# Lightning attention and a two-layer MLP on one core: the third pair of chunks as two units, with natural token order, later output stores and whole visits

## The chip, the cores and the metric

The kernel runs on one core of one Trainium2 chip. The metric is the device time of one execution in microseconds. The core's engines work side by side, each on its own queue in a fixed order: TensorE (PE, matmuls, with its weight loads as PEld), VectorE (DVE), ScalarE (ACT), GpSimd (POOL) and SyncE (SP), which only issues DMAs here. An engine that waits at the head of its queue holds up all that is queued behind it. Sixteen DMA engines serve all queues together.

## What is computed

The reference first does a causal linear attention with a decay per head, on q, k, v of shape (4, 8, 768, 64), in blocks of 64 tokens with a running state, and then an MLP on the 3,072 tokens with 512 channels:

```python
for b in range(nb):                      # blocks of 64 tokens
    intra = einsum('bhic,bhjc->bhij', qb, kb) * Dmask
    intra = einsum('bhij,bhjd->bhid', intra, vb)
    inter = einsum('bhid,bhde->bhie', qb * lam_pow, kv_state)
    out[:, :, sl] = intra + inter
    kv_state = lam_block * kv_state + einsum('bhsd,bhse->bhde', kb * rev_pow, vb)
...
h = x @ w_in                             # x: 3072 x 512, w_in: 512 x 2048
g = where(h >= 1, h, where(h <= -1, 0, (h + 1)**2 / 4))
out = g @ w_out                          # w_out: 2048 x 512
```

The kernel scales q by lam to the power of the position and k by its inverse (position counted from the middle of the sequence), so that the decays vanish from scores and state, and it computes in bf16 with fp32 sums.

## The kernel before

**Tiles and stages.** The tokens of the four sequences are cut into 24 chunks of 128 (6 to a sequence) and six stages of 512 tokens. For a stage, `f_l1` (L621) forms ph = w_in^T xT in pieces of 512 columns, `f_r` (L629, ACT) writes relu(h + 1) out of PSUM, `f_g` (L637, L640, L645, DVE) makes the activation gT, `f_l2` (L654) sums y over 16 pieces of gT and w_out, `f_y` (L679, ACT) copies y to an output buffer osb, and `f_out` (L686, L688 from POOL's queue, L690 and L675 from SP's) stores it. There are eight osb buffers (OB), two PSUM banks of ph and two of py: the copy of y number n + 8 needs the store of y number n to have landed, and an L621 group needs the L629 of the group two before it.

**Attention in units.** Tokens 0 to 511 (the first four chunks) come as four units of 256 tokens by 4 heads: unit 0 and 1 are the two head halves of tokens 0 to 255, units 2 and 3 of tokens 256 to 511. A unit is loaded with two neighbouring tokens side by side, in 512-byte runs (`e_load`, L317), so token 2p + j lies in partition p. It goes through scaling (`e_cast`, L330), transposes (`e_t`, L344), copies (`e_tc`, L351), scores (`e_s`, L388), mask (`e_m`, L396), state updates into the PSUM bank pu (`e_upd`, L364), copies of the state (`e_st`, L379), the state's part of the output (`e_sp`, L408), a drain of TensorE for units 2 and 3, the scores' part (`e_o`, L423), and a copy of the result to xT (`e_x`, L434). The tokens of a unit stand in xT with all even ones before all odd ones, and the stores of stage 0 put them back: each is two DMAs of 64 rows (L686).

**Chunks 4 and 5** (tokens 512 to 767, the end of the first sequence) are loaded by `f_load` (L441) in 256-byte runs, one head's row of one token each. k is scaled on DVE and q on POOL (L465), v cast on ACT (L458); `f_t` (L476) transposes on TensorE, `f_tc` copies (L481), `f_s` (L571) makes scores, `f_m` (L578) masks them, and `f_o` (L586, L590, L595) makes the output and, for chunk 4, the state update. `f_x` (L610) copies the output to xT, `f_ub` (L606) the state.

**Chunks 6 to 23** are loaded in the same 256-byte runs; k and q are scaled on POOL (L468), v cast on ACT (L458), and one DMA on SP's queue transposes k and q together (`f_tx`, L485, kqT). TensorE handles them in visits: `f_visit2(c)` multiplies scores by v (L542), adds the state's part (`f_sp`, L526), and then does `f_ahead(c + 1)`: `f_sp` and the scores of the next chunk (`f_sd`, L507) and the key-value products of the one after (`f_kv`, L515). DVE adds these up (`f_st`, L552 and L554), ACT casts the state (`f_sc`, L559), DVE masks the scores (L580), ACT copies the output (`f_xh`, L563). For c in SPLIT = (9, 11), `f_ahead` is a visit of its own some groups later.

**The order of the work.** A planner (`run_plan`) gives each piece an engine, a cost, needs and a due time, and from that writes down one order for every queue. What it emits is fixed; on the chip only the semaphores of the tiles and of the buffers count, so a need that stands only in a piece's list orders the plan and adds no wait. SP's queue holds all loads in order, with the transposes of kqT between them; a load of chunk c reuses the buffer of chunk c - 6. The first load of chunk 4 is held until the last but one slice of w_out has landed. POOL's queue holds the casts of k and q and the stores of stages 0 to 4; GL, LDMA, Y_TO and the like are the planner's numbers. The projections of stage 1 run in four parts of 128 tokens, those of stages 0 and 2 to 5 in two.

Of the kernel before, what the change touches and what calls it, by code (L numbers as in the profile page):

```python
# [23 lines left out]
def kernel(  # L24
# [16 lines left out]
    nc = tc.nc  # L41
# [13 lines left out]
    NU = 4  # L55
# [4 lines left out]
    XT, MG, NQT, NQK, NVS, NUB, RING = 6, 6, 4, 4, 5, 4, 3.5  # L60
# [36 lines left out]
    NE = 4  # L97
    pos_ei = const.tile([128, 2, 2], I32)
    nc.gpsimd.iota(pos_ei, pattern=[[2 * C, 2], [1, 2]], base=-S // 2, channel_multiplier=2)
# [208 lines left out]
    def get_ub(c):  # L308
        if c not in ubt:
            ubt[c] = ubp.tile([128, HP, D], BF16, name="ub", tag="ub")  # L310
        return ubt[c]

    def e_load(u, x):
        sc, r = divmod(u, 2)
        t = ld.tile([128, HR, 2 * D], F32, name=f"x{x}f", tag=f"x{x}f")
        s0 = sc * 2 * C
        ld_dma["e", u, x] = nc.sync.dma_start(  # L317
            out=t, in_=(q, k, v)[x][0, HR * r:HR * r + HR, s0:s0 + 2 * C, :].rearrange("h (p j) d -> p h (j d)", j=2))
        qkv_ld["e", u, x] = t

    def e_cast(u, x, eng):
        sc, r = divmod(u, 2)
        nm, dct = (("qs", qs), ("ks", ks), ("vs", vs))[x]
        t = qkp.tile([128, 2, HR, D], BF16, name=nm, tag=nm)
        dct["e", u] = t
        src = qkv_ld["e", u, x].rearrange("p h (j d) -> p j h d", j=2)
        if x == 2:
            (nc.scalar.copy if eng is nc.scalar else eng.tensor_copy)(t, src)
        else:
            eng.tensor_tensor(t, src, _bc(tab_e[x][:, 2 * sc:2 * sc + 2, HR * r:HR * r + HR], 3, D), op=AX.mult)  # L330
# [16 lines left out]

    def e_tc(u, i, eng):
# [7 lines left out]
    def e_upd(u, a):  # L356
        r, after = u % 2, a == 0 and u > 0
# [13 lines left out]
    def e_st(u, a, eng):  # L371

        if u >= NU:
            dst = get_ub(NU - 1)[:, 2 * (u % 2):2 * (u % 2) + 2, :]
        else:
            t = ubt["e", u, a] = ubp.tile([128, 2, D], BF16, name="ue", tag="ue", bufs=4)
            dst = t
# [21 lines left out]
    def e_sp(u):  # L399
        sc = u // 2  # L400
        po = pot["e", u] = [pp_y.tile([128, MS], F32, name="py", tag="py")[:, 0:256].rearrange("p (h q) -> p h q", h=2)
                            for _ in range(2)]
# [9 lines left out]
        e_upd(u, 1)  # L412

    def e_o(u):
        sc, po, after = u // 2, pot["e", u], u < NU - 2
# [15 lines left out]
    def e_x(u, a, eng):  # L431
        sc, r = divmod(u, 2)
        off = 2 * C * sc + C * a
        (nc.scalar.copy if eng is nc.scalar else eng.tensor_copy)(  # L434
            get_xT(0)[:, 2 * r:2 * r + 2, off:off + C], pot["e", u][a])


    def f_load(c, x, wait):
# [3 lines left out]
        if wait is not None:  # L442
            tc.add_manual_dep(d.ins, w_dma[wait].ins.name, SYNC)
# [8 lines left out]
    def pair(t, hp):  # L452
        return t[:, 2 * hp:2 * hp + 2, :].rearrange("p a d -> p (a d)")

    def cast(c, x, eng):
        if x == 2:
            t = vs[c] = qkp.tile([128, H, D], BF16, name="vs", tag="vs")
# [6 lines left out]
        if c < NCB:  # L464
            eng.tensor_tensor(t, qkv_ld[c, x], tb, op=AX.mult)  # L465
        else:
            h4 = "p (g i) d -> p g i d"
            eng.tensor_tensor(t.rearrange("p (i g) d -> p g i d", g=2), qkv_ld[c, x].rearrange(h4, g=2),  # L468
                              tb.rearrange(h4, g=2), op=AX.mult)

    def f_t(c):
        ptt[c] = (pp_o.tile([128, 2, HP, 128], BF16, name="po", tag="po") if c == NU
                  else pp_s.tile([128, 2, HP, 128], BF16, name="ps", tag="ps"))
        for i, x in ((1, ks), (0, qs)):
            for hp in range(HP):
                nc.tensor.transpose(out=ptt[c][:, i, hp, :], in_=pair(x[c], hp), identity=ident)  # L476

    def f_tc(c, i):
        dct, nm = ((qT, "qT"), (kT, "kT"))[i]
        t = dct[c] = qtp.tile([128, HP, 128], BF16, name=nm, tag=nm)  # L480
        nc.vector.tensor_copy(t, ptt[c][:, i])  # L481
# [83 lines left out]
    def f_s(c):  # L565
        for par in range(2):
            pst[c, par] = pp_s.tile([128, HP, 128], F32, name="ps", tag="ps")
        for hp in range(HP):
            for par in range(2):
                for a in range(2):  # L570
                    nc.tensor.matmul(pst[c, par][HD[a], hp, :], lhsT=kT[c][HD[par], hp, HD[a]],  # L571
                                     rhs=qT[c][HD[par], hp, :], start=True, stop=True, skip_group_check=True)

    def f_m(c, par):
        if par == 0:
            sc_sb[c] = scp.tile([128, 2, HP, 128 if c < NCB else 64], BF16, name="sc" if c < NCB else "sd", tag="sc" if c < NCB else "sd")
        if c < NCB:
            nc.vector.tensor_tensor(sc_sb[c][:, par], pst[c, par], _bc(causal, 1, HP), op=AX.mult)  # L578
        else:
            nc.vector.tensor_tensor(sc_sb[c][:, par], pst[c, par], _bc(diag, 1, HP), op=AX.mult)  # L580

    def f_o(c):
        po = pot[c] = pp_o.tile([128, HP, 128], F32, name="po", tag="po")
        for hp in range(HP):
            for par in range(2):
                nc.tensor.matmul(po[HD[par], hp, :], lhsT=ubt[c - 1][HD[par], hp, :], rhs=qT[c][HD[par], hp, :],  # L586
                                 start=hp == 0, stop=False, skip_group_check=True)
        for hp in range(HP):
            for par in range(2):
                nc.tensor.matmul(po[HD[par], hp, :], lhsT=vs[c][:, 2 * hp + par, :], rhs=sc_sb[c][:, par, hp, :],  # L590
                                 start=False, stop=True, skip_group_check=True)
        if c % NCB < NCB - 1:
            for hp in range(HP):
                for par in range(2):
                    nc.tensor.matmul(pu[0][HD[par], hp, :], lhsT=ks[c][:, 2 * hp + par, :], rhs=vs[c][:, 2 * hp + par, :],  # L595
                                     start=False, stop=True, skip_group_check=True)

    def f_visit(c):
        if c + 1 == NCB:
            f_kv(c + 1, get_sk())  # L600
        elif MG <= c + 1:
            f_s(c + 1)
        f_o(c)

    def f_ub(c):
        nc.scalar.copy(out=get_ub(c), in_=pu[0])  # L606

    def f_x(c):
        s, off = c // CPS, (c % CPS) * C
        nc.scalar.copy(out=get_xT(s)[:, :, off:off + C], in_=pot[c])  # L610
# [70 lines left out]
    def f_out(s, ms):  # L681
        m0 = s * MS + ms * 128
        if s == 0:

            for j in range(2):
                nc.gpsimd.dma_start(out=out[m0:m0 + 128, :].rearrange("(p j) n -> j p n", j=2)[j], in_=osb[s, ms][HD[j], :])  # L686
        elif s < NST - 1:
# [44 lines left out]
    GL = {(NU, 1): 7}  # L732
    LDMA, LDMB, TSP, TDMA = 1350, 80, 2000, 1300
    Y_TO = 9
    SPLIT = (9, 11)
    VSLACK, VSTEP, VS0, FSLACK = 2500, 700, 9, 1000
    XSLACK, LATE, LSTEP, OSLACK, OLATE, VQ = 400, 3000, 400, 1500, 12000, 12
# [6 lines left out]
    for u in range(NU):  # L744
        for x in (0, 1, 2):
            add(("ld", "e", u, x), "SP", 590, lambda u=u, x=x: e_load(u, x), [last_ld], due=pos_ * 1e-3, dma=880, ring=0.5)
# [183 lines left out]
```

## Time and profile before

| what | value |
|---|---|
| time, median of 3 runs (lowest to highest) | 209.11 us (208.47 to 209.81) |
| profiled execution: its time, its span | 207.5 us, 205.8 us |
| granted TensorE clock | 1.0 in all slices |
| busy: PE, PEld, DVE, ACT, POOL | 196.9, 135.7, 140.8, 120.4, 72.3 us |
| chain that ended last: PE, SP's queue, DMA, issue | 91%, 3%, 3%, 2% of the span |
| DMA | 94,909 packets, 34.48 MB; 82,210 packets under 512 bytes |
| SP's and ACT's DMA queues | 88,464 packets, 24.65 MB |
| loads of q, k, v (72 of 256 KB) | 4.8 to 5.6 us from issue to landing |
| stores on POOL's queue | 4.0 us (256 KB), 4.6 us (128 KB) |

The span goes from the first to the last instruction; the time holds some 1.7 us more. A row of a timeline gives the start and the length in us, then engine, line, operation, what is written and read, and how many instructions were merged; in brackets stands the idle time of the engine before it and what ended it. TensorE's matmuls overlap, so the starts of successive matmuls, not their lengths, tell the pace. The record of a matmul can be missing.

### The profile page before, as it was taken

To read this page: it belongs to the slowest core of one execution; us is meant where nothing else is said; L and a number is where in the kernel's file an instruction comes from. 1 tells how busy PE (TensorE), PEld (TensorE's weight loads), DVE (VectorE), ACT (ScalarE), POOL (GpSimd) and SP (SyncE) were. 2 spreads that over 40 slices of the span, in tenths; PEclk is the share of its full clock that TensorE was granted. 3 is DMA by queue.
4 is the path that set the end of the run, shared out by engine and by line. 5 is a ranking of instruction groups with operands and counts; after the bars stand their busy time and mean duration, and the time that the engine had idled before them with its cause. 6 is when DMAs were issued, how large, how long until landed. Compare 5 with 4: busy or idle time off the path is not lost.

```text
span 205.8 us, 6360 instructions
## 1 busy us (share of the span) xinstructions
PE 196.9 (96%) x2721; PEld 135.7 (66%) x2753; DVE 140.8 (68%) x251; ACT 120.4 (59%) x225; POOL 72.3 (35%) x95
## 2 busy tenths in 40 slices
PE   7789999999999999999999999999999999999994
PEld 2558875457867867767757777766766766666643
DVE  4694997254885985859985998978876656364510
ACT  4476763327676756675674877486585465463421
POOL 6898000264225363474365255445331011010000
PEclk9999999999999999999999999999999999999999
DMA  5999999999999999999999999999942011011112
GB/s 163 301 235 196 198 206 212 219 220 183 132 183 247 138 201 208 258 195 243 193 183 292 173 218 253 194 180 275 204 109 74 3 43 62 0 51 54 51 51 102
DMA packets 94909, 34.48 MB, mean 168 GB/s; under 512 B 82210, under 2 KB 93218, under 8 KB 94882
## 3 DMA queue, kind: packets, MB, share of 16 engines
q1 hardware_dynamic: 88464, 24.65, 70.5%
q0 software_dynamic: 6416, 9.44, 20.6%
q8 instruction: 21, 0.34, 0.7%
q14 instruction: 6, 0.05, 0.1%
q10 hardware_dynamic: 2, 0.00, 0.0%
HBM read 27.26 MB, written 6.29 MB: 163 GB/s over the span
## 4 chain that ended last, share of the span: by engine, by line
PE 91%; SPq 3%; DMA 3%; issue 2%; DVE 0%; ACT 0%
PE ph L621 41%; PE py L654 38%; SPq L317 3%; DMA x1f<-in_k_dram 3%; PE py L664 2%; PE ps L515 1%; PE py L621 1%; PE ps L507 1%; PE pu L542 1%; PE po L542 1%; PE po L526 1%; PE py L423 1%; PE pu L526 0%; DVE ks L330 0%; PE ps L571 0%
## 5 line engine op out<-in xcount | busy, mean ns | idle before, releaser
L621 PE MATMUL ph<-xT,w_in_sb 128*128 128x256 bf16 (+1 forms) x872 | 94.0, 257 | 0.0
L629 ACT ACTIVATE r<-ph,one 128x512 bf16<-128x512 f32 x93 | 63.8, 687 | 45.2 <-PE ph L621 38.7
L621 PEld LDWEIGHTS <-w_in_sb 128*128 128x128 bf16 x896 | 76.3, 98 | 19.6 <-issue 0.2
L654 PE MATMUL py<-w_out_sb,gT 128*128 128x512 bf16 x338 | 86.0, 379 | 2.3 <-issue 1.1
L654 PEld LDWEIGHTS <-gT 128*128 128x128 bf16 x368 | 34.9, 98 | 28.4
L637 DVE TENSOR_SCALAR t<-r 128x1024 bf16<-128x1024 bf16 x48 | 22.5, 468 | 32.8 <-ACT r L629 32.4
L645 DVE TENSOR_TENSOR gT<-w,t 128x1024 bf16<-128x1024 bf16 x48 | 39.0, 812 | 1.4
L640 DVE TENSOR_TENSOR w<-r,t 128x1024 bf16<-128x1024 bf16 x48 | 38.8, 808 | 1.6
L468 POOL TENSOR_TENSOR kq<-x1f,tkd 128x512 bf16<-128x512 f32 x18 | 20.4, 1131 | 33.2 <-DMA x1f<-in_k_dram 23.4
L468 POOL TENSOR_TENSOR kq<-x0f,tqd 128x512 bf16<-128x512 f32 x18 | 19.7, 1093 | 23.8 <-DMA x0f<-in_q_dram 23.7
L688 POOL DMA_DIRECT2D out_dram<-osb x16 | 9.2, 573 | 32.6 <-ACT osb L679 32.6
L679 ACT COPY osb<-py 128x512 f32<-128x512 f32 x23 | 13.5, 585 | 11.3 <-PE py L654 6.9
L580 DVE TENSOR_TENSOR sd<-ps,diag 128x256 bf16<-128x256 f32 x36 | 13.5, 417 | 3.7 <-PE ps L515 3.5
L458 ACT CAST vs<-x2f 128x512 bf16<-128x512 f32 x20 | 12.4, 618 | 4.9 <-DMA x2f<-in_v_dram 4.5
L554 DVE TENSOR_TENSOR st<-st,ps 128x256 f32<-128x256 f32 x30 | 12.5, 415 | 0.5
L559 ACT CAST us<-st 128x512 bf16<-128x512 f32 (+1 forms) x18 | 10.4, 579 | 1.3 <-DVE st L554 1.2
L465 POOL TENSOR_TENSOR kq<-x0f,tqd 128x512 bf16<-128x512 f32 x2 | 2.4, 1178 | 20.8 <-DMA x0f<-in_q_dram 20.8
L563 ACT CAST xT<-po 128x256 bf16<-128x256 f32 x18 | 6.8, 377 | 4.5 <-PE pu L526 4.0
L563 ACT CAST xT<-pu 128x256 bf16<-128x256 f32 x18 | 6.7, 374 | 2.3 <-PE po L526 2.3
L542 PEld LDWEIGHTS <-vs 64*64 64x64 bf16 x288 | 3.7, 107 | 6.5 <-issue 5.9
L396 DVE TENSOR_TENSOR sc<-ps,mask 128x512 bf16<-128x512 f32 x8 | 5.2, 682 | 2.1 <-PE ps L388 2.1
L515 PE MATMUL ps<-vs,kq 64*64 64x64 bf16 x264 | 6.2, 196 | 0.0
(96 smaller groups left out, 134.3 us busy)
## 6 DMA issues: line engine op xcount, KB each, us to landing
x0f<-in_q_dram SPq DMA_DIRECT2D x24, 256.0 KB, 5.6
x1f<-in_k_dram SPq DMA_DIRECT2D x24, 256.0 KB, 4.8
x2f<-in_v_dram SPq DMA_DIRECT2D x24, 256.0 KB, 5.4
out_dram<-osb POOLq DMA_DIRECT2D x16, 256.0 KB, 4.0
w_out_sb<-in_moe_w_out_dram POOLq DMA_DIRECT2D x4, 512.0 KB, 14.4
w_in_sb<-in_moe_w_in_dram POOLq DMA_DIRECT2D x3, 512.0 KB, 7.8
out_dram<-osb POOLq DMA_DIRECT2D x8, 128.0 KB, 4.6
out_dram<-osb SPq DMA_DIRECT2D x3, 256.0 KB, 2.0
```

Source lines behind the costliest of these rows:

```text
L458: (nc.scalar.copy if eng is nc.scalar else eng.tensor_copy)(t, qkv_ld[c, x])
L468: eng.tensor_tensor(t.rearrange("p (i g) d -> p g i d", g=2), qkv_ld[c, x].rearrange(h4, g=2), tb.rearrange(h4, g=2), op=AX.mult)
L554: nc.vector.tensor_tensor(st[c][:, a], st[c][:, 0] if a else st[c - 1][:, 1], kv[c][a], op=AX.add)
L563: nc.scalar.copy(out=get_xT(s)[:, :, off:off + 64], in_=po_of(c, a))
L580: nc.vector.tensor_tensor(sc_sb[c][:, par], pst[c, par], _bc(diag, 1, HP), op=AX.mult)
L621: nc.tensor.matmul(ph[:, j * m:(j + 1) * m], lhsT=w_in_sb[:, ko, (ni + j) * 128:(ni + j + 1) * 128], rhs=xT[s][:, ko, part * m:(part + 1) ...
L629: nc.scalar.activation(out=r_t[grp][:, i, :], in_=ph_t[s, ni, part], func=AF.Relu, bias=one[:, 0:1])
L637: nc.vector.tensor_scalar(t_t[grp], r, 0.5, 1.0, op0=AX.mult, op1=AX.min)
L640: nc.vector.tensor_tensor(w_t[grp], r, t_t[grp], op=AX.subtract)
L645: nc.vector.tensor_tensor(gT[s][:, f - RW * n:f, part * m:(part + 1) * m], w_t[grp].rearrange("p a (b m) -> p (a b) m", m=m), t_t[grp].rea ...
L654: nc.tensor.matmul(py_t[s, ms], lhsT=gT[s][:, ko, ms * 128:(ms + 1) * 128], rhs=w_out_sb[:, ko, :], start=(ko == 0), stop=(ko == FO - 1))
L679: nc.scalar.copy(out=osb[s, ms], in_=py_t[s, ms])
```

## The change

- Tokens 512 to 767 are units 4 and 5 (NS = 4 units as before, NU = 6 in all): loaded in 512-byte runs, transposed by one `e_t2` per unit, with the same scores, mask and output as the other units. Unit 4 forms its output in the two ph banks, unit 5 in the banks po and pu. Only the first of the two state updates is needed. The functions `f_t`, `f_tc`, `f_s`, `f_o`, `f_visit`, `f_ub` and `f_x` of chunks 4 and 5 go. The products `f_kv` of chunk 6 follow unit 5's output.
- `e_x` writes the tokens of all units to xT in natural order, with a step of two elements, and the stores of stage 0 are one DMA each.
- In the plan a store comes after visit min(y + 11, 23) and after the store before it.
- SPLIT is empty: visits 9 and 11 are whole.

The plan then comes out anew, so pieces of all queues move among each other.

```diff
-    NU = 4
+    NS, NU = 4, 6
...
-    NE = 4
-    pos_ei = const.tile([128, 2, 2], I32)
+    NE = 2 * (NU // 2)
+    pos_ei = const.tile([128, NU // 2, 2], I32)
...
+    def e_t2(u):
+        t = pp_o.tile([128, 2, 2, 2, 128], BF16, name="po", tag="po")
+        for i in (1, 0):
+            ptt["e", u, i] = t[:, i]
+            for j in range(2):
+                for hp in range(2):
+                    nc.tensor.transpose(out=t[:, i, j, hp, :],
+                                        in_=(qs, ks)[i]["e", u][:, j, 2 * hp:2 * hp + 2, :].rearrange("p a d -> p (a d)"),
+                                        identity=ident)
...
     def e_sp(u):
         sc = u // 2
-        po = pot["e", u] = [pp_y.tile([128, MS], F32, name="py", tag="py")[:, 0:256].rearrange("p (h q) -> p h q", h=2)
-                            for _ in range(2)]
+        if u < NS:
+            po = [pp_y.tile([128, MS], F32, name="py", tag="py") for _ in range(2)]
+        elif u == NS:
+            po = [pp_h.tile([128, MS], F32, name="ph", tag="ph") for _ in range(2)]
+        else:
+            po = [pp_o.tile([128, MS], F32, name="po", tag="po"), pp_u.tile([128, MS], F32, name="pu", tag="pu")]
+        po = pot["e", u] = [t[:, 0:256].rearrange("p (h q) -> p h q", h=2) for t in po]
...
-        e_upd(u, 1)
+        if u < NS:
+            e_upd(u, 1)
...
     def e_o(u):
-        sc, po, after = u // 2, pot["e", u], u < NU - 2
+        sc, po, after = u // 2, pot["e", u], u < NS - 2
         if not after:
             nc.tensor.drain()
...
-            get_xT(0)[:, 2 * r:2 * r + 2, off:off + C], pot["e", u][a])
+            get_xT(sc // 2)[:, 2 * r:2 * r + 2, off:off + C].rearrange("p h (q j) -> p h j q", j=2),
+            pot["e", u][a].rearrange("p h (j q) -> p h j q", j=2))
...
     def f_out(s, ms):
         m0 = s * MS + ms * 128
-        if s == 0:
-
-            for j in range(2):
-                nc.gpsimd.dma_start(out=out[m0:m0 + 128, :].rearrange("(p j) n -> j p n", j=2)[j], in_=osb[s, ms][HD[j], :])
-        elif s < NST - 1:
+        if s < NST - 1:
             nc.gpsimd.dma_start(out=out[m0:m0 + 128, :], in_=osb[s, ms])
...
-    SPLIT = (9, 11)
+    SPLIT = ()
...
+    for u in range(NS, NU):
+        od = l_due[1, 1, 0, 0] - LEAD - (3000 if u == NS else 0)
...
+        add(("s", "e", u), "PE", 400, lambda u=u: (e_s(u), e_upd(u, 0)),
...
+        add(("o", "e", u), "PE", 700 + (130 if u == NU - 1 else 0), lambda u=u: (e_sp(u), e_o(u), f_kv(NU, get_sk()) if u == NU - 1 else None),
...
             add(("st", y), "POOL" if s < NST - 1 else "SP", 800 if s < NST - 1 else 550, lambda a=(s, ms): f_out(*a),
-                [("y", y), ("o", 9 + y)] if s == 0 else [("y", y), ("st", y - 1) if y > CPS else None],
+                [("y", y), ("st", y - 1) if y else None, ("o", min(y + OGATE, NCH - 1)) if s < NST - 1 else None],
```

## The prediction

> **What bounds the kernel now.** I read the page from the top, then the waits of TensorE, then the order of time around the parts that change. Parts 1 and 2 first:
>
> ```profile
> PE 196.9 (96%) x2721; PEld 135.7 (66%) x2753; DVE 140.8 (68%) x251; ACT 120.4 (59%) x225; POOL 72.3 (35%) x95
> PE   7789999999999999999999999999999999999994
> PEclk9999999999999999999999999999999999999999
> DMA  5999999999999999999999999999942011011112
> ```
>
> TensorE is full from the fourth slice to the end, at full granted clock; the DMA engines are full for three quarters of the span. From 16 us on, the list of TensorE's waits holds one row:
>
> ```profile
> PE py L654 <- issue: 1.1, 7, 0.2
> ```
>
> That row is no wait for data: seven gaps of 0.16 where the first matmul record after a change of tile size is missing. So the end is 16 us of start plus TensorE's own work. An edit counts if it adds or removes TensorE time, or if something TensorE needs comes too late. The profiled execution took 207.5 us (span 205.8 and 1.7 around it); the three runs shown have a median of 209.11. Sums go against 207.5; I then add the difference of 1.6.
>
> **TensorE's work for tokens 512 to 767.** I call 2,048 moving columns of the two projections a group: 4 matmuls of L654 at 0.216, or 8 of L621 at 0.109, each 0.87 us (16 of 128 columns take 0.895). Times of attention stretches are from the start of the next projection matmul back to the start of the last plus its pitch, less 0.216 where a record is missing. Before, the two chunks take 0.45 (8 transposes), 0.44 (scores), 1.35 (transposes and output of chunk 4), 0.45 (scores) and 0.91 (output of chunk 5 with L515): 3.61 us. After, the instruction order gives four stretches of unit work, priced by the rows of units 2 and 3. Transposes: 0.45. Scores, 8 state updates, transposes: 0.44 + 0.16 + 0.45 = 1.05; 0.16 is L364 x8 from 15.90 to 16.18 less the way out. The third has state, drain and output of unit 4, then scores and updates of unit 5: unit 3's stretch took 1.09 from 17.06 to 18.14 with 8 updates, so 0.93 without them, plus 0.25 (scores, 15.65 to 15.90) plus 0.16 = 1.34. The last is 0.93 + 0.15 (L515 x16) = 1.08. Sum 3.92: **+0.31**. Of that the two new drains are most: in unit 3 the output matmuls start 0.31 after the last update. Bounds: 0 if the drains find TensorE empty, +0.6 if each stretch also pays a change of tile size. I take +0.3.
>
> **No split visits.** Visits 9 and 11 were cut in two:
>
> ```profile
> 74.96 1.03 PE L654 MATMUL py<-w_out_sb,gT 128*128 128x512 bf16 x4
> 75.92 0.22 PE L542 MATMUL po<-sd,vs 64*64 64x64 bf16 x2
> ...
> 76.23 1.90 PE L654 MATMUL py<-w_out_sb,gT 128*128 128x512 bf16 x7
> 77.97 1.91 PE L621 MATMUL ph<-xT,w_in_sb 128*128 128x256 bf16 x16
> 79.81 0.22 PE L526 MATMUL po<-kqT,us 64*64 64x64 bf16 x2
> ...
> 80.02 0.29 PE L515 MATMUL ps<-vs,kq 64*64 64x64 bf16 x8
> ```
>
> The columns are start, length, engine, line, operation. Four L654 from 74.96 end their turn at 75.82, the next projection starts at 76.23: 0.41. Sixteen L621 from 77.97 end at 79.71, the next starts at 80.24: 0.53. Uncut visits with the same matmuls take 0.72 (163.55 less 162.84), so the cut cost 0.21; for visit 11 it is 0.95 against 0.77, 0.17. **-0.38**. What is late next: the second halves now need their inputs in the first visit.
>
> **A stall that goes.** In the run of 64 L621 from 50.60 two matmuls started 0.10 and 0.20 late (52.49, 53.59), while ScalarE did a v cast and L559 between two L629. In the new order ScalarE has five L629 in a row there: **-0.3**, or 0 if they bunch again.
>
> **Loads and moved visits.** The position of each visit among the groups changes: chunk 6's first stretch from 38 groups to 34, visits 6, 7, 8, 9 from 44, 49, 56, 59 to 41, 47, 52, 59 (the last now whole), visits 12 and 13 from 83 and 90 to 80 and 86, equal from visit 16 on. So inputs are wanted up to 3.5 us earlier. Against that, the six loads of chunks 4 and 5 get 512-byte runs. Twelve such loads at the start landed from 3.76 to 13.98, 0.93 apart; the twelve from 33.01 on, of 256-byte runs, from 36.77 to 50.44, 1.24 apart. Six times 0.31 is **1.9 us earlier** for everything behind them on SP's queue (bounds: 0, if the second dozen was slow for another reason such as the queue's 2.44 us issue at 44.79; 1.9). The Trainium skill speaks against so much: DMA: Bandwidth & Descriptors, "Why small descriptors are slow", has a fixed cost of about 3 cycles per packet beside one per 32 bytes, so 19 cycles where two short packets take 22; by it a load would go from 1.24 to 1.07, an estimate, six would save 1.0, and the wait worked out below would be 1.2 instead of 0.3.
>
> The tightest place is visit 6. Before:
>
> ```profile
> 57.78 0.62 ACT L559 CAST us<-st 128x512 bf16<-128x512 f32 x1
> 58.84 0.62 ACT L458 CAST vs<-x2f 128x512 bf16<-128x512 f32 x1 [0.44 <-DMA x2f<-in_v_dram]
> ```
>
> The v of chunk 8 landed at 58.82, and the visit began at 60.25. After, it begins three groups earlier (2.65), with +0.3 and -0.3 from above: 57.6; its first use of chunk 7's state is some 0.3 in, at 57.9. The v lands at 56.9, its cast ends at 57.6, and L559 of chunk 7 is now *behind* that cast on ScalarE's queue: 58.2, with a semaphore 0.1 more. **+0.3** (0 to 1). The earlier places come out even: unit 5's state copy, behind chunk 6's v cast on ScalarE, is ready near 47.0 against a use near 47.1; chunk 6's kqT (51.47 less 1.9) against 50.8. At visit 8 the v of chunk 10 (71.64 less 1.9, less one store of 1.1 that no longer precedes it) is cast by 69.3 against a start at 69.3.
>
> **Stores.** The new gate is only in the plan; on the chip a store waits for its copy and for its place on GpSimd's queue, which moves behind 19 chunk casts: the first store from 63.1 to after the cast of chunk 15's k. Eight output buffers exist, so the ninth L679 waits for the first store, the tenth for the second, and every L629 behind it on ScalarE waits too. The tenth has its input after 87 groups, near 104.6. The second store is behind the k cast of chunk 16:
>
> ```profile
> 106.35 1.14 POOL L468 TENSOR_TENSOR kq<-x1f,tkd 128x512 bf16<-128x512 f32 x1 [1.87 <-DMA x1f<-in_k_dram]
> 107.44 1.15 POOL L688 DMA_DIRECT2D out_dram<-osb  x2
> ```
>
> From chunk 6's k (43.95) that is 6.24 per chunk with stores among the loads; the three chunks without (43.95 to 61.12) took 5.72 each. At 5.72, less 1.9, the cast starts at 99.3 and ends at 100.4; the store lands 4.0 later (the median of these), 104.4. **0**, with 0.2 of room on ScalarE and some 1.5 before TensorE runs out of L621 results to overwrite. The half stores of tokens 0 to 511 become whole: one issue of 0.58 for two of 0.55, on an engine at 35%.
>
> **Natural order.** The copies out of the units write bf16 at a step of two elements. No row of before writes so; the nearest are these copies as they are, 0.37 (ACT) and 0.42 (DVE), L434. Bounds: no change to doubled. The copy on DVE, 18.29 to 18.71, feeds a matmul at 19.03: doubled it costs 0.1. I take 0, the same number of elements. The Trainium skill (SBUF — State Buffer, the note on cachelines) allows eight bf16 of step for free; no run here shows it. Tables of 48 instead of 32 columns lie beside the loads: the start ends with the k load of unit 3, landing at 13.13.
>
> **Sum.** +0.3 - 0.4 - 0.3 + 0.3 + 0 + 0 = **-0.1**, and about -0.3 if visit 6 finds its inputs. I take -0.2: 207.3 for an execution like the profiled one, **208.9** beside the median. Bounds of the terms (TensorE 0 to +0.6, stall -0.3 to 0, visit 6 0 to 1) give 208.4 to 210.3.
>
> **Rivals.** *Slower, loads late (0.13):* the 1.9 does not come. Then visit 6 waits for 58.82 + 0.62 + 0.62 + 0.1 = 60.2 against 57.9: +2.2 in place of +0.3, **210.9**, a little under 1%; with less v first. The full DMA row speaks for it, the two spacings against. *Slower, output buffers (0.13):* TensorE waits behind the tenth L679. It decides from a pace over 5.9 us per chunk; at the old 6.24 the second store lands at 109.6, 5 us late, 3.5 after ScalarE's room: **212.5**. For it: casts 20 to 23 came 5.93 apart with few stores. Against: these were not bound by stores alone. *Faster (0.16):* the runs shown are 1.0 to 2.3 above the profiled execution; chunk 13's kqT landed at 99.47 for a visit that began at 99.38, so a slightly later load stalls there. With stores out of the way that chunk comes some 5 us earlier for a visit 2.65 earlier, and the runs would lose such stalls: 207.5 - 0.5 = **206.9**. Nothing shown says that those runs stalled. That the change does not do what it says is the first rival.
>
> **Numbers.** Forecast 0.58, faster 0.16, late loads 0.13 (0.04 of it within 1%), buffers 0.13. One per cent, 2.1 us, is about what a measurement can tell. Faster 0.16, same 0.62, slower 0.22. The range takes the faster case and the late loads with a bound on each: 206.5 to 211.8.
>
> **What would show it.** Right: under-512-byte packets down by 6,144; the six loads 0.9 apart; no TensorE wait over 0.5 after 20 us; whole visits 9 and 11 at 0.7 to 0.8; four unit stretches summing to 3.9. Wrong: TensorE waiting by over 1 near 57.9 for the state cast of chunk 7, L629 held behind an output copy near 105, unit copies over 0.6.

## The result: a little slower

The changed kernel took 209.07 us in the median of 20 runs (208.56 to 210.86), the kernel before 208.40 (20 runs, 207.72 to 209.81): a ratio of 1.0044, 95% interval 1.0028 to 1.0060. That is 0.9 us more. The forecast of 208.9 stood for a gain of 0.2 on an execution like the profiled one, and it was set against a median of three runs that lay 0.7 above this one. The time is near the number and inside the range, but that is luck: the direction is wrong, the change costs 0.4%, and no bound was set for what costs it. A step that the prediction priced at nothing is the cause.

The profiled execution of the changed kernel took 208.97 us with a span of 207.3, against 207.5 and 205.8. The page of the changed kernel, parts 1 and 2:

```profile
PE 200.1 (97%) x2777; PEld 136.9 (66%) x2777; DVE 139.6 (67%) x251; ACT 120.7 (58%) x228; POOL 69.7 (34%) x91
PE   7698999999999999999999999999999999999994
PEclk9969999999999999999999999999999999999999
DMA  4999999999999999999999999996932002011112
```

TensorE is as full as before from the fifth slice on. The extra 1.5 us of span are 0.75 ahead of the first projection matmul (16.93 against 16.18), 0.76 between the first and the last projection matmul (187.32 against 186.56), and nothing behind it. The 0.75 lies in the start, where the third slice shows a lower granted clock (0.64 in the mean from 10 to 13 us), and the experiments below show a start that scatters as much without the change. The 0.76 is the subject. TensorE's waits from 16 us on, where the profile of the kernel before had no wait for data, are now (columns: waiting tile and line, what ended the wait, total, times, longest):

```profile
PE py L569 <- ACT xT L443: 0.5, 1, 0.5
PE py L416 <- ACT ue L382: 0.2, 1, 0.2
```

L569 is the first projection (L621 before), L443 the copy of a unit's result into xT (L434 before), L382 the copy of the state (L379 before), L416 the state's part of the output. The timeline of the changed kernel at that place, TensorE, ScalarE and VectorE, with the idle time before an instruction and its releaser in brackets:

```profile
16.93 1.05 PE L569 MATMUL ph<-xT,w_in_sb 128*128 128x256 bf16 x8
17.80 0.44 ACT L443 CAST xT<-py 128x256 bf16<-128x256 f32 x1 [0.80 <-PE ph L569]
...
18.10 0.27 ACT L382 CAST ue<-pu 128x128 bf16<-128x128 f32 x1
...
18.43 0.24 PE L416 MATMUL py<-qT,ue 64*64 64x128 bf16 x2 [0.22 <-ACT ue L382]
...
19.30 1.05 PE L569 MATMUL ph<-xT,w_in_sb 128*128 128x256 bf16 x8
20.39 0.44 ACT L443 CAST xT<-py 128x256 bf16<-128x256 f32 x1 [1.19 <-PE ph L569]
20.39 0.44 DVE L443 CAST xT<-py 128x256 bf16<-128x256 f32 x1 [2.19 <-PE ph L569]
20.88 1.03 PE L569 MATMUL py<-xT,w_in_sb 128*128 128x256 bf16 x8 [0.53 <-ACT xT L443]
```

The same place in the timeline of the kernel before:

```profile
18.14 1.05 PE L621 MATMUL ph<-xT,w_in_sb 128*128 128x256 bf16 x8
18.24 0.37 ACT L434 CAST xT<-py 128x256 bf16<-128x256 f32 x1
18.29 0.42 DVE L434 CAST xT<-py 128x256 bf16<-128x256 f32 x1 [0.89 <-PE py L423]
19.03 1.04 PE L621 MATMUL py<-xT,w_in_sb 128*128 128x256 bf16 x8
```

Read the brackets. Before, the copies of unit 3 wait for L423, the matmuls that make what they copy, and lie beside the second projection group. After, they wait for **L569, a projection**, which reads the columns of tokens 0 to 255, while the copies write tokens 256 to 511. No data passes between the two. The third group, which does need the copies, starts 0.695 late (20.88 less the start of the second at 19.30, less the 0.88 from one group's start to the next without a wait, to the rounding of the rows). The same happens one step earlier: unit 2's second copy waits at the head of ScalarE's queue until the first group is nearly through (17.80), behind it stands the state copy L382 of unit 3 (18.10), and for that TensorE waits. Unit 3's stretch, from the end of the first group to the start of the second, becomes 1.49 where it was 1.086: 0.41 more. Together **1.10 us**. Everything else of the change gave -0.34, and 1.10 - 0.34 is the 0.76 found.

This sum stands on one profile of each kernel, and on that of the kernel before it was lucky. A second profile of the kernel before has 187.22 between its first and last projection matmul, nearly as much as the changed kernel, because TensorE waited 0.66 for a slice of w_in that had landed in time in the first one (until 21.82). What the change costs is therefore read from the medians, and what causes it from the experiments.

### The profile page after: what moved, and what is told of

The parts are those of the page before. It is cut to its first block, busy times and chain, and to the rows that moved or that the text cites. A ratio compares the mean times of both kernels' runs of the same rounds, so it can differ in the third digit from the quotient of the medians.

```text
span 207.3 us, 6444 instructions
## 1 busy us (share of the span) xinstructions
PE 200.1 (97%) x2777; PEld 136.9 (66%) x2777; DVE 139.6 (67%) x251; ACT 120.7 (58%) x228; POOL 69.7 (34%) x91
## 2 busy tenths in 40 slices
DMA packets 91773, 34.48 MB, mean 166 GB/s; under 512 B 76002, under 2 KB 90082, under 8 KB 91746
## 4 chain that ended last, share of the span: by engine, by line
PE 95%; ACT 1%; DVE 1%; POOL 1%; issue 0%
PE ph L569 40%; PE py L602 39%; PE py L612 2%; PE ps L505 1%; PE py L569 1%; PE ph L115 1%; PE ps L497 1%; PE po L532 1%; PE pu L532 1%; PE ps L391 1%; PE py L432 1%; POOL qs L327 1%; PE ph L341 1%; PE pu L371 1%; PE po L516 1%; PE po L341 1%
## 5 line engine op out<-in xcount | busy, mean ns | idle before, releaser
L569 PE MATMUL ph<-xT,w_in_sb 128*128 128x256 bf16 (+1 forms) x872 | 94.3, 257 | 0.0
L602 PE MATMUL py<-w_out_sb,gT 128*128 128x512 bf16 x368 | 91.7, 379 | 0.0
L569 PEld LDWEIGHTS <-w_in_sb 128*128 128x128 bf16 x896 | 76.5, 98 | 20.5 <-issue 0.7
L602 PEld LDWEIGHTS <-gT 128*128 128x128 bf16 x368 | 35.0, 98 | 27.3
L585 DVE TENSOR_SCALAR t<-r 128x1024 bf16<-128x1024 bf16 x48 | 24.7, 515 | 33.2 <-ACT r L577 32.7
L593 DVE TENSOR_TENSOR gT<-w,t 128x1024 bf16<-128x1024 bf16 x48 | 37.5, 782 | 1.3
L588 DVE TENSOR_TENSOR w<-r,t 128x1024 bf16<-128x1024 bf16 x48 | 37.3, 778 | 1.6
L470 POOL TENSOR_TENSOR kq<-x0f,tqd 128x512 bf16<-128x512 f32 x18 | 20.2, 1120 | 20.8 <-DMA x0f<-in_q_dram 20.6
L632 POOL DMA_DIRECT2D out_dram<-osb x20 | 11.2, 561 | 37.0 <-ACT osb L627 37.0
L327 POOL TENSOR_TENSOR qs<-x0f,tqe 128x512 bf16<-128x512 f32 x6 | 6.8, 1141 | 21.3 <-DMA x0f<-in_q_dram 20.7
L399 DVE TENSOR_TENSOR sc<-ps,mask 128x512 bf16<-128x512 f32 x12 | 7.8, 686 | 6.8 <-PE ps L391 6.7
L463 ACT CAST vs<-x2f 128x512 bf16<-128x512 f32 x18 | 11.0, 613 | 1.0 <-DMA x2f<-in_v_dram 1.0
L115 PE MATMUL ph<-zz 128*128 128x512 bf16 (+1 forms) x14 | 5.7, 543 | 1.3 <-DVE zz L103 1.3
```

What stands on the lines that cost most here:

```text
L569: nc.tensor.matmul(ph[:, j * m:(j + 1) * m], lhsT=w_in_sb[:, ko, (ni + j) * 128:(ni + j + 1) * 128], rhs=xT[s][:, ko, part * m:(part + 1) ...
L585: nc.vector.tensor_scalar(t_t[grp], r, 0.5, 1.0, op0=AX.mult, op1=AX.min)
L588: nc.vector.tensor_tensor(w_t[grp], r, t_t[grp], op=AX.subtract)
L593: nc.vector.tensor_tensor(gT[s][:, f - RW * n:f, part * m:(part + 1) * m], w_t[grp].rearrange("p a (b m) -> p (a b) m", m=m), t_t[grp].rea ...
L602: nc.tensor.matmul(py_t[s, ms], lhsT=gT[s][:, ko, ms * 128:(ms + 1) * 128], rhs=w_out_sb[:, ko, :], start=(ko == 0), stop=(ko == FO - 1))
L632: nc.gpsimd.dma_start(out=out[m0:m0 + 128, :], in_=osb[s, ms])
```

## The experiments

All ratios are to the kernel before, run on the same chip in turn; they come from 10 to 12 runs of each kernel and 17 to 35 of the kernel before. "Stretch" is unit 3's stretch, "late" the delay of the third projection group, both from the profiled execution.

| kernel | order in xT, form of the copy | stretch, late (us) | ratio, 95% interval |
|---|---|---|---|
| after, again | natural, step 2 in xT | 1.490, 0.695 | 1.0039, 1.0016 to 1.0062 |
| before + natural order | natural, step 2 in xT | 1.494, 0.695 | 1.0037, 1.0009 to 1.0065 |
| after, split view | natural, step in PSUM, pairs | 1.456, 0.624 | 1.0019, 0.9993 to 1.0044 |
| the same, two tables | natural, step in PSUM, pairs | 1.455, 0.624 | 1.0035, 1.0016 to 1.0055 |
| after, two xT tiles | natural, step 2 in xT | 1.085, 0 | 1.0002, 0.9978 to 1.0026 |
| the same, two tables | natural, step 2 in xT | 1.085, 0 | 1.0009, 0.9984 to 1.0035 |
| after, even/odd order | even/odd, plain | 1.085, 0 | 0.9997, 0.9967 to 1.0028 |
| after, plain view | natural, step in PSUM, plain | 1.085, 0 | 1.0003, 0.9977 to 1.0029 |
| before + natural, plain view | natural, step in PSUM, plain | 1.084, 0 | 0.9991, 0.9967 to 1.0015 |

The two groups do not mix: where the copies wait for the projections the ratio is 1.002 to 1.004, where they do not it is 0.999 to 1.001. The intervals of single rows overlap. Clearest are the four kernels that ran beside each other, 12 runs each: medians of 209.20 and 209.24 us with the wait (the changed kernel, natural order alone), 208.33 and 208.31 without it (two tiles, even/odd order). Now one by one.

### The changed kernel again, two xT tiles, even/odd order, and natural order alone

*The changed kernel again*, for a profile beside the others:

> The changed kernel once more, beside the three kernels that follow and on their chip. Every theory: its ratio to the kernel before stays near 1.0044. The profile tells whether the start of the projections (first L569 at 16.93 in the first profile, 16.18 before) is late again, and whether the first cast on POOL takes 1.5 again: if either is gone here, it belongs to that execution and not to the change.

*Two tiles.* Each stage's xT becomes two tiles of 256 tokens; instructions, orders and the stepped copies stay:

```diff
-            xT[s] = xp.tile([128, KO, MS], BF16, name="xT", tag="xT")
+            xT[s, half] = xp.tile([128, KO, MS // 2], BF16, name="xT", tag="xT")
...
-            get_xT(sc // 2)[:, 2 * r:2 * r + 2, off:off + C].rearrange("p h (q j) -> p h j q", j=2),
+            get_xT(sc // 2, sc % 2)[:, 2 * r:2 * r + 2, off:off + C].rearrange("p h (q j) -> p h j q", j=2),
...
```

> The changed kernel with xT in two tiles of 256 tokens per stage instead of one of 512; same instructions, same order on every queue, the copies still write with a step of two elements. Theory A (a wait that the data do not need: a copy with three free dimensions is taken to overlap the projection's reads in the same tile): the copies of units 2 and 3 no longer wait for L569, the third projection group loses its 0.7 us gap and unit 3's stretch falls from 1.49 to about 1.1; ratio to before 0.999 (1.1 us less than the changed kernel). Theory B (the stepped write itself is slow, 0.44 a copy against 0.37): nothing moves by more than 0.1, ratio stays 1.0044. Theory C (the late start comes from what precedes the copies, casts, loads or clock): ratio stays 1.0044 as well, with the copies' waits gone.

*Even/odd order.* The units' results go to xT as before the change, even tokens ahead of odd ones, now for all six units, with half stores for these tokens; the rest is the changed kernel:

```diff
-            get_xT(sc // 2)[:, 2 * r:2 * r + 2, off:off + C].rearrange("p h (q j) -> p h j q", j=2),
-            pot["e", u][a].rearrange("p h (j q) -> p h j q", j=2))
+            get_xT(sc // 2)[:, 2 * r:2 * r + 2, off:off + C], pot["e", u][a])
...
```

> The changed kernel with the even and odd order of tokens kept in all six units and two half stores for each of the six 128-token tiles of tokens 0 to 767; all else and the orders of the queues as changed. Theory A: as with the split tiles, ratio 0.999, copies at 0.37 without waits for L569. Theory B: 0.999 too. Theory C: 1.0044. More POOL time for the half stores (0.55 each, six more) should cost nothing.

*Natural order alone.* The kernel before with the stepped copy and whole stores of stage 0:

> The kernel before with one part of the change alone: the copies out of the four units write the tokens in natural order, and stage 0's stores are one DMA each. Theory A: the second copy of unit 2 and both of unit 3 wait for the projection's matmuls, 0.4 + 0.7 = 1.1 us, ratio 1.005. Theory B: 0.1 to 0.2 us, ratio 1.001. Theory C: 1.000.

Measured: 1.0039 and 1.0037 for the changed kernel and for natural order alone, 1.0002 and 0.9997 for two tiles and for even/odd order. Natural order on its own makes the whole difference, and taking it back or moving the other tokens into a tile of their own removes it. The timeline of the kernel with two tiles:

```profile
19.06 1.05 PE L569 MATMUL ph<-xT,w_in_sb 128*128 128x256 bf16 x8
19.16 0.45 ACT L443 CAST xT<-py 128x256 bf16<-128x256 f32 x1
19.20 0.45 DVE L443 CAST xT<-py 128x256 bf16<-128x256 f32 x1 [0.83 <-PE py L432]
19.94 1.04 PE L569 MATMUL py<-xT,w_in_sb 128*128 128x256 bf16 x8
```

The copies are as long as in the changed kernel (0.45) and nothing is late: it is not their length. And the same place in the kernel before with natural order alone:

```profile
18.44 0.45 ACT L434 CAST xT<-py 128x256 bf16<-128x256 f32 x1 [1.59 <-PE ph L622]
...
21.59 1.03 PE L622 MATMUL py<-xT,w_in_sb 128*128 128x256 bf16 x8 [0.53 <-ACT xT L434]
```

So theory B (the stepped write is slow) and theory C (a late start of something before) fall for the 0.44%. Theory A stands: a wait that the data do not need.

### Which form of the copy makes the wait

Two forms keep natural order in one tile and move the step to the PSUM side. In the first the written view is still split into pairs:

```diff
-            get_xT(sc // 2)[:, 2 * r:2 * r + 2, off:off + C].rearrange("p h (q j) -> p h j q", j=2),
-            pot["e", u][a].rearrange("p h (j q) -> p h j q", j=2))
+            get_xT(sc // 2)[:, 2 * r:2 * r + 2, off:off + C].rearrange("p h (q j) -> p h q j", j=2),
+            pot["e", u][a].rearrange("p h (j q) -> p h q j", j=2))
```

> Natural order as in the changed kernel, in one xT tile per stage, but the copy out of a unit writes its 128 tokens of a head one behind the other and takes the step of 64 on its PSUM side. Same instructions, same orders. Theory A (only the stepped write with its three free dimensions is taken to touch columns of the next head's other tokens): the copies do not wait for projections, unit 3's stretch is 1.09 instead of 1.49, the third projection group is not 0.7 late, ratio to before 1.000 (0.998 to 1.002), 0.4% below the changed kernel. Rival A2 (natural order in a shared tile waits however it is written): 1.004, stretch 1.49. The length of the copies: 0.37 to 0.45 on ScalarE if a step in PSUM is free, more if it is not.

Measured: 1.0019, stretch 1.456, third group 0.624 late. My sharper version of theory A, that it takes a stepped write, fell: this copy writes 128 tokens one behind the other and still waits. Its ratio alone would not show it, as the interval holds 1; its timeline does:

```profile
17.29 0.37 ACT L443 CAST xT<-py 128x256 bf16<-128x256 f32 x1 [0.88 <-PE ph L569]
...
20.27 1.03 PE L569 MATMUL py<-xT,w_in_sb 128*128 128x256 bf16 x8 [0.46 <-ACT xT L443]
```

The copy on ScalarE is back at 0.37, and the two waits are 0.1 shorter together. In the second form only the written view is stated differently, as two rows of 128 tokens (a row of xT holds the tokens of one pair of heads):

```diff
-            get_xT(sc // 2)[:, 2 * r:2 * r + 2, off:off + C].rearrange("p h (q j) -> p h q j", j=2),
+            get_xT(sc // 2)[:, 2 * r:2 * r + 2, off:off + C],
```

> As the kernel with the contiguous write (natural order, one xT tile, the step on the PSUM side), but the written view is given plainly as two heads of 128 tokens, not split into 64 pairs per head. The instruction writes the same addresses in the same order; only the form in which the program states the view differs. Theory A3 (a view stated as many short runs is taken for all that lies between its first and last element, so the copy is made to wait for readers of the next head's other tokens): no wait, unit 3's stretch 1.09, the third projection group on time, ratio to before 0.998 to 1.001. Rival A2 (natural order in a shared tile waits in any form): stretch 1.4, third group 0.7 late, ratio 1.002 to 1.004 as measured with the split view.

Measured: 1.0003, no wait at this place. Its timeline:

```profile
16.53 0.65 ACT L443 CAST xT<-py 128x256 bf16<-128x256 f32 x2 [0.39 <-PE py L432]
...
18.88 1.05 PE L569 MATMUL ph<-xT,w_in_sb 128*128 128x256 bf16 x8
18.98 0.37 ACT L443 CAST xT<-py 128x256 bf16<-128x256 f32 x1
19.02 0.42 DVE L443 CAST xT<-py 128x256 bf16<-128x256 f32 x1 [0.83 <-PE py L432]
...
19.76 1.04 PE L569 MATMUL py<-xT,w_in_sb 128*128 128x256 bf16 x8
```

Same engine, same addresses in the same order, same length; the copies now wait for L432, which makes their data. On the kernel before the plain form does the same:

> The kernel before with natural token order and whole stores of stage 0, as measured once at 1.0037 with the stepped write, but with the plainly stated contiguous write. Theory A3: no wait, ratio 0.999 to 1.001. Rival A2: 1.003 to 1.004 again, third projection group 0.7 late.

Measured: 0.9991 against the 1.0037 of the stepped form. So the wait comes from the form in which the program states the written view, when its waits are laid down: a view of many short runs (in each partition 256 runs of one element in the stepped form, 128 of two in the split one) is handled as if it covered what lies between its first and last element. In each partition, xT has four rows of 512 tokens for a stage; unit 2 writes in the first two, unit 3 in the last two, and between the two pieces that a copy writes lie tokens 0 to 255 of its second row.

The timeline of the changed kernel speaks for this, and against a copy that waits for all readers of the tile. A projection group reads rows one to four twice, its matmuls 0.109 apart, so its sixth matmul is the last to read row two and its eighth the last to read row four. Unit 2's second copy starts 0.87 after its group (17.80 less 16.93), unit 3's copies 1.09 after theirs (20.39 less 19.30): two matmuls later. That the number of runs is the point, and where the limit lies, was not measured; shown is that these two split forms wait and the plain form does not.

### Is the late start part of the change?

The first q cast on GpSimd took 1.04 in the profile of before and 1.51 in that of after, and the first projection came 0.75 later. The tables of 48 columns in place of 32 shift that cast by 0.03, so two kernels compute the table of units 0 to 3 alone first:

```diff
-    tab_e = tables(pos_e, NE, "e")
+    tab_e = tables(pos_e[:, 0:NS], NS, "e")
...
     tab = tables(pos, NCB, "d")
+    tab_e2 = tables(pos_e[:, NS:NE], NE - NS, "e2")
...
```

> The kernel with the contiguous write, and the table of units 0 to 3 computed alone with 32 columns as before the change; 16 columns for units 4 and 5 follow behind the tables of the chunks. Theory S (48 columns make the first q cast on GpSimd start 0.03 to 0.05 later, beside the k cast on VectorE, and that costs the start): first q cast 1.04 instead of 1.5 to 1.6, first scores near 7.5 instead of 8.0 to 8.2, first projection 0.3 to 0.8 earlier than with 48 columns, ratio to before 0.996 to 0.998. Rival L (the start is set by when the loads land, the slow cast has room): first projection unchanged, 16.9 to 17.1, ratio as with the contiguous write alone, 1.000.

> The kernel with two xT tiles per stage and stepped copies, with the same split table. Theory S: first q cast 1.04, first projection 0.3 to 0.8 earlier than the 17.09 seen with 48 columns, ratio to before 0.996 to 0.998. Rival L: 1.000, as with two tiles alone (1.0002), first projection near 17.

> The kernel before, once more, for the scatter of its start. Ratio 1.000. Theory S: first q cast 1.04, first projection near 16.2 as in its first profile. Rival L: the first projection scatters by 0.5 or more between profiles of one kernel, with the landing of the loads, so it may come near 16.9.

Measured: the cast took 1.04 in both, but the ratios did not fall: 1.0035 against 1.0019 with the split view, 1.0009 against 1.0002 with two tiles. The first projection came at 16.45 and 16.37, and in the second profile of before at 16.56. In the second profile of the changed kernel the late start and the long cast were there again (17.12 and 1.60). Theory S, which asked for 0.002 to 0.004 less, is not borne out, though the intervals are as wide as that. The kernel before, run again beside them, came out at 0.9993 (0.9971 to 1.0015). Over all the profiles the first projection lies between 16.18 and 17.87 in kernels built on the one before, and between 16.37 and 17.12 in those built on the changed one. It goes roughly with the landing of the third load, which is issued at 1.86 in each: landed at 5.95, it was 16.18 (before); at 6.40, 16.93 (after); at 6.91, 17.09 (two tiles); at 7.45, 17.55 (the kernel before with whole visits, below). One does not fit: 6.33 and 17.87 (natural order with whole visits, below), where TensorE ran at a slower pace through the start. The start scatters without the change as much as with it. Rival L fits better, and the start is left out of what follows.

### Whole visits alone, and with natural order

> The kernel before with SPLIT empty and nothing else changed. If the term is right: visits 9 and 11 whole at 0.72 and 0.73 to 0.79, 0.38 to 0.42 less TensorE time, ratio 0.998. Rival: the second half's inputs (scores' kqT and the state of the chunk after) come too late for the earlier place, because here the loads have not become earlier: a wait of 0.3 to 1 at visit 9 or 11, ratio 1.000 to 1.003.

```diff
-    SPLIT = (9, 11)
+    SPLIT = ()
```

Measured: 1.0001, 0.9978 to 1.0024. Visits 9 and 11 are whole at 0.717 and 0.729, as forecast. Of the 0.42 that this saves, 0.36 came back in the same profile: two gaps of 0.126 and 0.116 between projections (86.72, 103.12) and 0.12 at the start of a later visit (105.74). Together with natural order in the plain form:

> The kernel before with two parts of the change: natural order and whole stores with the plainly stated contiguous write, and SPLIT empty; chunks 4 and 5 stay as they were, without the 0.20 of TensorE work that the two more units add. By the sums of the profiles: visits 9 and 11 give 0.4, nothing waits for the copies, ratio 0.998, the body from the first to the last projection 186.1 to 186.4 against 186.55. Rival: the 0.4 is eaten by late inputs and small stalls at the moved visits, as with SPLIT empty alone (1.0001), ratio 0.9995 to 1.001.

Measured: 1.0007, 0.9987 to 1.0026: no gain either, and 186.70 between the first and the last projection where 186.1 to 186.4 was forecast. The same two gaps are there (0.126, 0.114), and a third of 0.33. The timeline of this kernel shows what the third is:

```profile
62.92 0.69 DVE L641 TENSOR_TENSOR w<-r,t 128x1024 bf16<-128x1024 bf16 x1
...
64.93 1.03 POOL L469 TENSOR_TENSOR kq<-x1f,tkd 128x512 bf16<-128x512 f32 x1 [1.28 <-DMA x1f<-in_k_dram]
64.98 1.54 DVE L646 TENSOR_TENSOR gT<-w,t 128x1024 bf16<-128x1024 bf16 x1
...
66.58 1.04 PE L655 MATMUL py<-w_out_sb,gT 128*128 128x512 bf16 x4 [0.17 <-DVE gT L646]
```

A cast on GpSimd started 0.05 ahead of VectorE's L646, which then took 1.54 instead of 0.69, and the second projection waited. When the cast starts depends on when its load lands. None of the kernels tried beats the kernel before by more than its interval.

## Why the prediction was wrong

| step of the prediction | forecast (us) | measured in the profile of after |
|---|---|---|
| units' TensorE work, four stretches | +0.31, sum 3.92 | 0.446 + 1.017 + 1.281 + 1.064 = 3.81, **+0.20** |
| no split visits | -0.38 | 0.717 and 0.730 whole, **-0.42** |
| the ph stall goes | -0.3 | 0.106 + 0.106 for 0.095 + 0.205, **-0.09** |
| visit 6 waits | +0.3 | no wait, **0** |
| output stores | 0 | no wait, **0** |
| natural order | 0 (up to 0.1) | 0.41 + 0.695, **+1.10** |
| sum, taken | -0.2 | 0.76 (0.79 by these rows) |

**The step that failed is "Natural order".** It asked only how long the copies would be, bounded that by "no change to doubled", and worked out 0.1 for a doubled copy. The length was nearly right: 0.45 for 0.37 on ScalarE and 0.44 for 0.42 on VectorE. What it did not ask is what the copy waits for, and who stands behind it. The prediction treated the edit as a price of an instruction, while it was an edit of an access, and every access in such a kernel decides which waits are written into the program. Neither bound could hold it. Of the prediction's own signs, "no TensorE wait over 0.5 after 20 us" is the one that failed, with 0.53 at 20.88. The row that was needed stood in the profile of before: `18.29 0.42 DVE L434` ran beside the projection of 18.14, so the copies of tokens 256 to 511 depended on being told apart from the reads of tokens 0 to 255 in the same tile. With that cover gone, the price follows from that timeline: the copy can start only after the second group and stands between it and the third.

**Units' work.** The mechanism is right and the sum 0.11 too high: 0.03 in the second stretch, 0.06 in the third, 0.02 in the last. Which of the rows added up was too dear was not followed up.

**Split visits.** Right to 0.04 in the changed kernel. Visit 9 in its timeline, one projection, one attention visit and the next projection:

```profile
76.91 1.03 PE L602 MATMUL py<-w_out_sb,gT 128*128 128x512 bf16 x4
77.87 0.22 PE L532 MATMUL po<-sd,vs 64*64 64x64 bf16 x2
...
78.27 0.29 PE L505 MATMUL ps<-vs,kq 64*64 64x64 bf16 x8
...
78.49 1.25 PE L602 MATMUL py<-w_out_sb,gT 128*128 128x512 bf16 x5
```

Four L602 from 76.91 end at 77.77, the next starts at 78.49. But the whole visits alone show that such a saving is not a time: other waits took most of it.

**The ph stall.** The forecast let it go entirely, since five L629 stood in a row; "0 if they bunch again" was the bound, and they did by two thirds.

**Loads.** The direction is right, the size is not. Packets under 512 bytes fell by 6,208 (82,210 to 76,002; 6,144 forecast). Five of the units' six loads have a landing in the trace, about 1.0 apart (37.30, 38.12, 39.24, 40.39, 41.28). From the first of the six to the load behind them it is 6.11 (37.30 to 43.41), before it was 7.11 (36.77 to 43.88): 1.0 saved and not 1.9. The 1.24 of the forecast was the mean over twelve loads with one late landing among them (45.02 to 47.55), next to the queue's long issue that the prediction named as its bound. By the rule of the Trainium skill (DMA: Bandwidth & Descriptors, "Why small descriptors are slow") six loads save 1.0, the prediction's estimate from that page; the trace agrees. The v of chunk 8 did land 2.2 earlier, counted from the first load of the batch (57.16 against 58.82, with a first load 0.53 later), so 1.2 of that came on loads that the change leaves as they were. That is in part luck: counted so, it landed after 19.9 to 22.0 in the six profiles of kernels built on the one before, the 22.0 being the profile that the prediction read, and after 18.9 to 20.2 in the eight built on the changed one.

**Visit 6.** The order on ScalarE is as foreseen, v cast of chunk 8, then the state cast of chunk 7 (rows of after):

```profile
57.65 0.61 ACT L463 CAST vs<-x2f 128x512 bf16<-128x512 f32 x1
58.16 0.62 ACT L549 CAST us<-st 128x512 bf16<-128x512 f32 x1
...
59.83 0.20 PE L516 MATMUL pu<-kqT,us 64*64 64x64 bf16 x2
```

But the first use came at 59.83 instead of 57.9: the start of this execution was 0.75 later, and the false wait added 1.10. In kernels without that wait the thin place shows, one visit on or at unit 5, as in the kernel with the plain view (row of its timeline):

```profile
65.07 0.14 PEld L516 LDWEIGHTS <-us 64*64 64x64 bf16 x8 [0.19 <-ACT us L549]
```

Visit 7 there took 1.018 instead of 0.788; with two tiles TensorE waited 0.77 at visit 7, with two tiles and two tables 0.40 at unit 5's state copy, with even/odd order nothing: 0.35 in the mean of the four. The four profiled executions with the false wait had 0.05 at most there. So the wait of 1.10 also served as cover for what came behind, and the -0.34 of the other parts is taken back by such stalls without it. Waits for weights may have been covered in the same way: two of the nine profiles without the false wait have them between 21 and 31 us (0.66 in the second profile of before; 1.12 in three gaps, two of them ended by landings of weights, in the kernel before with the plain view), none of the five with it. That fits the medians (1.000 without the false wait, 0.2 to 0.4% above it with), but it rests on one or two profiled executions of each kernel; how often the stalls come in the other runs stays open.

**Stores.** The second store landed at 100.90 and the tenth output copy started at 106.14 (forecast 104.4 and 104.6): more room than thought, since GpSimd made 5.25 us per chunk (43.54 to 96.02) and not 5.72. The k cast of chunk 16 and the second store in the timeline of after:

```profile
96.02 1.04 POOL L470 TENSOR_TENSOR kq<-x1f,tkd 128x512 bf16<-128x512 f32 x1 [2.25 <-PE ph L569]
97.00 0.60 POOL L632 DMA_DIRECT2D out_dram<-osb  x1
```

## What to carry to other kernels

Price a changed access pattern by its waits as well as by its length: list who else touches the same tile, ask whether the program can still tell the two apart, and look at who is queued behind the instruction that would wait. Where a view of many short runs is written into a tile that others read, state the written side as plain runs and put the step on the side that is read, or give the other tokens a tile of their own; the bracket of the instruction, naming a releaser that makes none of its data, is the sign. And a saving in a full engine's work is only an upper bound when its inputs arrive by loads with a spread of the same size.

## What the runs showed of the hardware that was not expected

- **VectorE and GpSimd hold each other up, whole instructions long.** In the profile of before, 16 of the 96 L640 and L645 (both operands bf16 in SBUF) started while a cast on GpSimd ran: 1.42 us in the median against 0.69 for the other 80. L637 goes from 0.43 to 0.82 in the median (five cases). L580 and L554, which read PSUM, do not change (0.41 to 0.42 in both cases). Whoever starts first is not held up: the first two casts in the kernel with the plain view,

```profile
4.82 1.04 POOL L327 TENSOR_TENSOR qs<-x0f,tqe 128x512 bf16<-128x512 f32 x1 [0.55 <-ACT tqe L139]
4.83 1.58 DVE L327 TENSOR_TENSOR ks<-x1f,tke 128x512 bf16<-128x512 f32 x1 [0.18 <-ACT tqe L139]
```

  and in the kernel before with whole visits:

```profile
4.77 0.69 DVE L330 TENSOR_TENSOR ks<-x1f,tke 128x512 bf16<-128x512 f32 x1
4.77 1.59 POOL L330 TENSOR_TENSOR qs<-x0f,tqe 128x512 bf16<-128x512 f32 x1 [0.51 <-ACT tqe L139]
```

  The Trainium skill (SBUF — State Buffer, "SBUF: two separate sides") describes a port pair that the first of the two to start holds for its whole instruction, where VectorE's operation has two SBUF inputs or runs in a two-port mode; the rows agree. The times of VectorE so depend on when loads land.
- **A step of 64 fp32 elements on the PSUM side costs the copy nothing** (0.37 on ScalarE, 0.42 on VectorE, as unstepped), a step of two bf16 elements on the SBUF side 0.07 to 0.08 on ScalarE. On VectorE that step cost 0.02 to 0.03. The Trainium skill (SBUF — State Buffer, the note on cachelines) has the latter free; nearly so on VectorE, but a fifth of the copy's time on ScalarE, and the measurement decides.
- **TensorE's pace in the start differs between executions** at full granted clock in the records: four transposes L344 took 0.40 us at 6.42 in one, 0.61 at 15.33 in another (before, and natural order with whole visits). In five of the fourteen profiles the records do show a lower clock in the start, and the pace follows it: with natural order alone it was 0.63 in the mean from 17 to 20 us, and the matmuls of the first projection group started 0.213 apart where they start 0.109 apart elsewhere. With the third load, these are further reasons for the spread of the start; they were not followed up.
